# A low-rank product U^T x in an attention kernel with two mixers: taken once a batch over 512 columns, where it was taken once a pair of heads over 128

## The chip, the cores and the metric

The kernel runs on one core of a Trainium2 chip, as one program of 12022 instructions. The metric is the device time of one execution in microseconds. TensorE is called PE below, its loading of weights PEld, VectorE DVE, ScalarE ACT, GpSimd POOL, and the queue on which nearly all transfers are issued SP.

## The reference

A clustered attention is followed by two mixers. Batch 2, 8 heads, 768 tokens, head size 64, so 512 channels.

```python
scores = where(q_assign == k_assign, q @ k^T / 8, -1e9)      # clusters from an argmax against 16 centroids
x = softmax(scores) @ v                                       # laid out as (batch, 768 tokens, 512 channels)
# first mixer: U is 768 x 32, V is 32 x 768
h = x^T @ U @ V
u = x + h^T
x = u + relu(u @ w_ch1) @ w_ch2                               # 512 -> 2048 -> 512
# second mixer
h = relu(x^T @ w_tok1) @ w_tok2                               # 768 -> 256 -> 768
u = x + h^T
out = u + relu(u @ w_ch1') @ w_ch2'                           # 512 -> 1536 -> 512
```

The change concerns the first factor of the token mixing, z = U^T x: for each batch a 32 x 512 matrix (32 ranks by 512 channels), summed over 768 tokens.

## The kernel before, in words

The eight heads of a batch are worked as four pairs; a pair fills 128 channels. There are G = 8 pairs in all (g = 0 to 3 are batch 0, g = 4 to 7 batch 1). The attention of a pair is cut into 9 tiles (NTT), so the whole attention is 72 steps (`step`, L587). A step n runs the exponential of tile n on ACT (L298), the score matmuls of tile n+1 on PE (`st_mm`, L287, groups qS<-kS in the trace, printed as ps<-qS,kS), the units that find the row maxima of the next pair (`max_unit`, L246, printed as ps<-kS,qS, each with a maximum on DVE at L258 or L260), the product with v of tile n-1 (`pv`, L303, ps<-vt,p), and then the list `late[n]`, which is filled by hand with `at(late, s, ...)` from L525 on. Every engine works its own instructions in the order in which they are written, so this list is the schedule.

The result of the attention is divided and stored into `xn` (`pv_out`, L316), whose layout is 128 partitions (a token within a block) by batch, pair, token block (6 of them, NS) and 128 channels. It is float32.

The low-rank product of pair g is `zmm(g)` (L327): 6 matmuls, one for each token block, with a 128 x 32 block of U as the weights (`u_sb`) and the 128 channels of the pair moving. Both are plain float32, which the trace shows as two PE instructions for each matmul, 12 a pair. It is written into one bank of PSUM. `zmm_out(g)` (L334) then copies it twice on ACT, to partitions 0 to 31 and 32 to 63 of `zst` (L337, L338), and puts the remainder of the rounding into partitions 64 to 95 on DVE (L339, recorded at L88). With its three parts `zst` is the moving side of `zadd(b, t)` (L342), which multiplies with V and adds to `xn` (`zadd_out`, L345).

`zmm(g)` stands in `late` of step 9g+10, that is in the second step of the next pair, and `zmm_out(g)` in the step after it, for g = 0 to 6. The bank is 6 + g % 2, one of the two that `pv` uses in turn. The product of the last pair, g = 7, is the first entry of `rest_of_u` (L779), a list whose entries are taken in turn with half units of the first mixer's channel matmuls (`hidden`, `outmm`, L626 to L653: 12 matmuls of 512 columns each). There is one `zadd` for each of a batch's six token blocks: those of batch 0 stand in the steps of pairs 5 to 7 (L570), the first at step 49, those of batch 1 in `rest_of_u`, the first two entries after the product.

Besides, `tick` (L517) puts in the conversion of the weights of the mixers, which arrive as 64-bit words (`conv_all`, L477 on): two ACT instructions, four on DVE, one on POOL and two transfers each time.

The PE instructions of all these functions are issued by the helper `mm` (L75), so the trace has them all at L76; they are told apart by their tiles.

Of the kernel before, what the change touches and what calls it, by code (L numbers as in the profile page):

```python
# [18 lines left out]
P = 128  # L19
# [5 lines left out]
def tile_cluster_attention__then__two_mixers(  # L25
# [25 lines left out]
    NB, NPAIR, _, S = qT.shape  # L51
    HS = S // 2
    NS = S // P
    NT = HS // P
    D = 64
    CD = NPAIR * P
    NC = CD // P
    NFA, NFB = wa.shape[0], wb.shape[0]
    R = U.shape[1]
    DT = wt1.shape[1]  # L60
    NDT = DT // P
    G = NB * NPAIR
# [10 lines left out]
    ps = psp.tile([P, 8, 512], F32, name="ps")  # L73

    def mm(o, l, r, start, stop, **kw):  # L75
        pe.matmul(o, lhsT=l, rhs=r, start=start, stop=stop, **kw)  # L76
# [10 lines left out]
    def sub(eng, o, a, b):  # L87
        eng.tensor_tensor(out=o, in0=a, in1=b, op=ALU.subtract)  # L88
# [30 lines left out]
    xn = fp.tile([P, NB, NPAIR, NS, P], F32, name="xn")  # L119
# [38 lines left out]
    u_sb = const.tile([P, NS, R], F32, name="u_sb")  # L158
    vst = const.tile([96, S], F32R, name="vst")
    zst = const.tile([96, NB * CD], F32R, name="zst")  # L160
# [3 lines left out]
    def load_pair(g, eng=sp):  # L164
        b, p = divmod(g, NPAIR)
        eng.dma_start(Rq, qT[b, p])
        eng.dma_start(Rk, kT[b, p])

    def load_v(g):
        b, p = divmod(g, NPAIR)  # L170
        for a in range(2):
            sp.dma_start(vt[g % 2][:, a, :, 0:D], v[b].rearrange("(c s) d -> s c d", s=P)[:, :, p * P + a * D : p * P + a * D + D])
# [4 lines left out]
    def ring():  # L177

        banks.append(banks.pop(0))
        return banks[-1]  # L180

    held = {}

    def scores(g, bk=None):

        p = g % NPAIR
        held["sc"] = bk = ring() if bk is None else bk
        for qd in range(4):
            src = (Rq, Rk)[qd // 2]
            mm(ps[32 * qd : 32 * qd + 32, bk, 0:HS], zc[:, ts(p, 32)], src[:, ts(qd % 2, HS)], True, True)  # L190
# [28 lines left out]
    def q_lo(eng, o):  # L219
        eng.scalar_tensor_tensor(out=o.bitcast(F32R), in0=Rq, scalar=0.125, in1=Hq, op0=ALU.mult, op1=ALU.subtract)  # L220

    def k_lo(eng, o):
        sub(eng, o.bitcast(F32R), Rk, Hk)
# [22 lines left out]
    def max_unit(g, m):  # L246
        a, r = divmod(m, 9)
        q, k = qS[g % NST][a], kS[g % NST][a]
        bk = ring()
        tp, w = divmod(r, 3)  # L250
        for j, (t, k0, n) in enumerate([(2 * tp + w, 0, 512)] if w < 2 else [(2 * tp, 512, 256), (2 * tp + 1, 512, 256)]):
            o = ps[:, bk, j * n : j * n + n]
            mm(o, q[0:KA, 0, ts(t, P)], k[0:KA, 0, k0 : k0 + n], True, False)
            mm(o, q[0:KB0, 1, ts(t, P)], k[0:KB0, 1, k0 : k0 + n], False, True)
        i = 6 * a + 2 * tp
        mxs = mxs_[g % 2]
        if w < 2:
            dve.tensor_reduce(out=mxs[:, i + w, 0:1], in_=ps[:, bk, :], axis=AX.X, op=ALU.max, negate=True)  # L258
        else:
            dve.tensor_reduce(out=mxs[:, i : i + 2, 1], in_=ps[:, bk, :].rearrange("p (t k) -> p t k", t=2),  # L260
                              axis=AX.X, op=ALU.max, negate=True)

    def max_rows(g, tps=None, eng=sp):

        i, n = (0, NT) if tps is None else (tps, 1)
        parts = lambda t: t.rearrange("p (a t w) -> p a t w", a=2, w=2)[:, :, i : i + n]
        dve.tensor_reduce(out=parts(mxz[:, 0:12]), in_=mxs_[g % 2].rearrange("p (a t w) c -> p a t w c", a=2, w=2)[:, :, i : i + n],
                          axis=AX.X, op=ALU.min)
        bk = ring()
        mm(ps[:, bk, 0:P], mxz, ident, True, True)  # L270
        o = ps[0:12, bk, 0:P]
        m = mr[i % 2]
        rnd(dve, m[0:12, 0, :].bitcast(F32R), o)
        sub(dve, m[0:12, 1, :].bitcast(F32R), o, m[0:12, 0, :])
        for a in range(2):
            for j in range(2):
                d = f32(qS[g % NST][a])[96 + j : 97 + j, 1, i * QB : (i + n) * QB].rearrange("o (t s) -> o t s", s=P)
                eng.dma_start(d, m[6 * a + 2 * i : 6 * a + 2 * i + 2 * n, j, :])
# [22 lines left out]
    OB = 6  # L301
# [14 lines left out]
    def pv_out(k):  # L316
        g, qb = divmod(k, NQB)
        b, p = divmod(g, NPAIR)
        o = ps[:, OB + k % 2, 0 : 4 * VW].rearrange("p (a t x) -> p a t x", a=2, x=VW)
        r = rr[k % 2]  # L320
        dve.tensor_scalar(out=r, in0=o[:, :, :, D], scalar1=EPS, scalar2=None, op0=ALU.add)
        dve.reciprocal(r, r)
        dve.tensor_tensor(
            out=xn[:, b, p, ts(qb, 2), :].rearrange("p t (a d) -> p a t d", a=2), in0=o[:, :, :, 0:D],
            in1=r.unsqueeze(3).to_broadcast([P, 2, 2, D]), op=ALU.mult)

    def zmm(g, bk=None):  # L327
        b, p = divmod(g, NPAIR)
        held["z"] = bk = ring() if bk is None else bk
        z = ps[0:R, bk, 0:P]  # L330
        for c in range(NS):
            mm(z, u_sb[:, c, :], xn[:, b, p, c, :], c == 0, c == NS - 1)

    def zmm_out(g):  # L334
        z = ps[0:R, held["z"], 0:P]
        o = zst[:, ts(g, P)]
        act.copy(o[0:32], z)  # L337
        act.copy(o[32:64], z)  # L338
        sub(dve, o[64:96], z, f32(o[0:32]))  # L339
# [183 lines left out]
    early, mid, late, mus = {}, {}, {}, {}  # L523

    def at(d, s, f):  # L525
        d.setdefault(max(s, 0), []).append(f)

    for g in range(G):
        s0 = NTT * g
        for qb in range(NQB):  # L530
            at(late, s0 + 3 * qb + 3, lambda k=NQB * g + qb: pv_out(k))
        if g + 1 < G:
            at(late, s0 + 10, lambda g=g: zmm(g, OB + g % 2))
            at(late, s0 + 11, lambda g=g: zmm_out(g))
            n1 = g + 1
            cnt = (2, 2, 2, 2, 2, 2, 2, 2, 2) if g > 1 else (3, 3, 3, 3, 3, 3) if g else (0, 0, 0, 0, 0, 3, 4, 4, 4, 3)
            m0 = 0
            for s, k in zip(range((-2, 0, -3)[min(g, 2)], 8), cnt):
                for m in range(m0, m0 + k):
                    at(mus, s0 + s, lambda g=n1, m=m: max_unit(g, m))  # L540
                m0 += k
            at(mid, s0 + (6 if g else 7), lambda g=n1: max_rows(g))
        if g + 2 < G:
            n2 = g + 2
            at(late, s0 - (4 if g > 1 else 3), lambda g=n2: load_pair(g))
            at(late, s0 + 10, lambda g=n2: load_v(g))
            s1 = s0 - 1 if g else 3
            at(late, s1 - 1, lambda g=n2, bk=OB + (3 * g if g else 1) % 2: scores(g, bk))
            at(late, s1 - 1, q_hi)
            at(late, s1, k_hi)  # L550
            at(late, s1, scores_out)
            at(late, s1, argmax_a)
            at(late, s1 + 1, argmax_b)
            at(late, s1 + 1, lambda: k_lo(pool, Rk))
            for a in range(2):
                at(late, s1 + 1, lambda g=n2, a=a: stack(g, a, "hi", sp))
                at(late, s1 + 3, lambda g=n2, a=a: stack(g, a, "lo", sp))
                at(late, s1 + 3, lambda g=n2, a=a: stack(g, a, "mask", sp))
            at(late, s1 + 2, mask_rows)
            at(late, s1 + 2, lambda: q_lo(dve, Rq))  # L560
        for s in (2, 4, 6) if g else (7, 8):
            at(late, s0 + s, tick)
# [7 lines left out]
    for t in range(NS):  # L570
        g, qb = 5 + t // 2, t % 2
        s, bk = NTT * g + 3 * qb + 4, OB + (NQB * g + qb) % 2
# [206 lines left out]
    def rest_of_u():  # L779


        ops = [(lambda bk: zmm(G - 1, bk), lambda bk: zmm_out(G - 1))]
        u_ = [(umm, umm_out, 0, t) for t in range(TW // P, NS)] + [(umm, umm_out, 1, t) for t in range(NS)]
        z_ = [(zadd, zadd_out, 1, t) for t in range(NS)]
        order = [x for p in zip(u_, z_) for x in p] + u_[NS:]
        for f, o, b, t in order:
            ops.append((lambda bk, f=f, b=b, t=t: f(b, t, bk), lambda bk, o=o, b=b, t=t: o(b, t, bk)))
        for i in range(len(ops) + 1):
            if i:
                ops[i - 1][1](6 + (i - 1) % 2)  # L790
            if i < len(ops):
                ops[i][0](6 + i % 2)
            yield
# [4 lines left out]
    def conv_rest():  # L798
        for k in range(2 * len(blocks)):
            if k % 9 % 2 or k % 9 == 0:  # L800
                tick()
            yield

    bg = [rest_of_u(), conv_rest()]
    while done < end(0, 2) - 24:
        for t in bg:
# [48 lines left out]
```

## Time and profile before

| | us |
|---|---|
| three runs | 866.0, 862.29, 870.77 (median 866.0) |
| the profiled execution's own time | 862.45 |
| its span in the trace | 860.4 |
| PE busy in the span | 815.7 |
| DVE, ACT, POOL busy | 457.5, 239.2, 121.1 |

The span is the time from the first to the last instruction of the profiled execution; about 2.0 us lie around it. A duration of a PE matmul in the trace holds the passage through the array, so successive matmuls overlap: the distance from one start to the next is what it costs the engine. In a timeline a row is a run of like instructions, with its start, its length and its count; an idle time before it stands in brackets, with what ended it. The granted clock is PE's share of its full 2.4 GHz: 0.50 is the lower level of 1.2 GHz, 1.00 the higher.

### The profile page before, as it was taken

The numbers are of one execution on the slowest core, as the hardware profiler recorded it, in microseconds if no ns is written. First come the engines' busy times: TensorE is split into PE (matmuls) and PEld (weight loads), VectorE is DVE, ScalarE is ACT, GpSimd is POOL, SyncE is SP. The second block draws the span as 40 slices with busy tenths as digits, with TensorE's granted clock in tenths as the row PEclk, the third lists the DMA queues.
The fourth block names the chain that finished last, engine by engine and source line by source line (L and its number), as shares of the span: only waits on it lengthen the run. The fifth ranks groups of instructions, "written<-read, shape, count | busy, mean of one in ns | idle before, by whom it ended". The sixth has DMA issues, their size and how long they took to land.

```text
span 860.4 us, 12022 instructions
## 1 busy us (share of the span) xinstructions
PE 815.7 (95%) x4585; PEld 702.6 (82%) x4585; DVE 457.5 (53%) x795; ACT 239.2 (28%) x367; POOL 121.1 (14%) x103
## 2 busy tenths in 40 slices
PE   0779899999999999999999999999999999999997
PEld 0668799999989999788888888888888888888886
DVE  3746667676767545877877588751242124113113
ACT  1221333434333334433323333321211121111010
POOL 3000001102111011212312332310210021000000
PEclk9998899999999999999999999999999999999999
DMA  8554735677774436799989999973454345754852
GB/s 212 126 118 127 164 111 139 200 168 220 179 191 133 165 101 208 284 358 333 376 292 321 416 388 417 402 265 137 130 171 166 127 130 162 250 193 163 275 191 80
DMA packets 70505, 184.72 MB, mean 215 GB/s; under 512 B 21776, under 2 KB 24016, under 8 KB 70448
## 3 DMA queue, kind: packets, MB, share of 16 engines
q1 hardware_dynamic: 69232, 181.83, 65.1%
q10 hardware_dynamic: 1216, 2.14, 1.0%
q8 instruction: 36, 0.59, 0.3%
q14 instruction: 21, 0.17, 0.1%
HBM read 130.88 MB, written 32.51 MB: 190 GB/s over the span
## 4 chain that ended last, share of the span: by engine, by line
PE 88%; DVE 5%; DMA 4%; SPq 2%; issue 1%; ACT 0%; ACTq 0%; DVEq 0%
PE ps L76 87%; DMA sq__101<-in_qT_dram 2%; DVE mxs L258 1%; DMA kS<-sk__102 1%; PE ps L731 1%; DMA whl<-scr_a 1%; DMA kS<-om 0%; PE ps L351 0%; SPq L239 0%; DMA cc<-in_cen_dram 0%; SPq L240 0%; DVE xn L663 0%; DVE mxs L260 0%; DVE ul L88 0%; DVE am L199 0%
## 5 line engine op out<-in xcount | busy, mean ns | idle before, releaser
L76 PE MATMUL ps<-uh,whl 128*128 128x512 f32 x672 | 223.1, 393 | 0.9 <-issue 0.9
L76 PE MATMUL ps<-gh,whl 128*128 128x512 f32 x672 | 222.1, 392 | 0.0
L641 DVE SCALAR_TENSOR_TENSOR gl<-ps,gh 128x512 fp32r<-128x512 f32 x84 | 58.0, 690 | 220.5 <-ACT gh L640 220.5
L76 PEld LDWEIGHTS ps<-uh,whl 128*128 128x128 f32 x672 | 126.2, 188 | 28.0 <-issue 1.1
L76 PEld LDWEIGHTS ps<-gh,whl 128*128 128x128 f32 x672 | 126.2, 188 | 27.2
L76 PE MATMUL ps<-vt,p 128*128 128x65 f32 x1152 | 138.6, 274 | 0.0
L76 PEld LDWEIGHTS ps<-vt,p 128*128 128x128 f32 x1152 | 137.2, 194 | 0.2
L76 PE MATMUL ps<-ul,whl 128*128 128x512 f32 x336 | 132.0, 393 | 1.0 <-DVE ul L88 1.0
L76 PE MATMUL ps<-gl,whl 128*128 128x512 f32 x336 | 132.0, 393 | 0.0
L640 ACT ACTIVATE gh<-ps 128x512 fp32r<-128x512 f32 x84 | 50.2, 598 | 288.7 <-PE ps L76 288.7
L88 POOL TENSOR_TENSOR chl<-c,chl 128x512 fp32r<-128x512 f32 x56 | 76.0, 1358 | 334.7 <-ACT chl L81 300.6
L298 ACT ACTIVATE p<-ps 128x1024 f32<-128x1024 f32 x72 | 73.2, 1021 | 136.9 <-PE ps L76 136.8
L76 PE MATMUL ps<-kS,qS 112*128 112x512 f32 (+3 forms) x384 | 87.0, 360 | 23.2 <-DMA kS<-om 17.0
L76 PE MATMUL ps<-qS,kS 112*128 112x256 f32 x576 | 98.6, 297 | 1.0 <-DMA qS<-mr 1.0
L258 DVE TENSOR_REDUCE mxs<-ps 128x1 f32<-128x512 f32 x96 | 63.6, 684 | 61.0 <-PE ps L76 60.8
L76 PEld LDWEIGHTS ps<-qS,kS 112*128 112x128 f32 x576 | 83.5, 195 | 11.5 <-issue 2.8
L76 PEld LDWEIGHTS ps<-kS,qS 112*128 112x128 f32 (+1 forms) x384 | 62.1, 202 | 32.6 <-issue 18.5
L76 PEld LDWEIGHTS ps<-ul,whl 128*128 128x128 f32 x336 | 63.2, 188 | 14.2 <-DVE ul L88 1.3
L76 PEld LDWEIGHTS ps<-gl,whl 128*128 128x128 f32 x336 | 63.2, 188 | 13.0
L81 ACT ACTIVATE chl<-c 128x512 fp32r<-128x512 f32 x56 | 35.3, 631 | 58.3 <-DMA scr_a<-chl 25.0
L107 DVE SCALAR_TENSOR_TENSOR c<-c,c 128x512 int32<-128x512 int32 (+1 forms) x63 | 47.4, 752 | 2.2
L106 DVE TENSOR_SCALAR c<-c 128x512 int32<-128x512 int32 (+1 forms) x63 | 45.7, 725 | 2.1
(113 smaller groups left out, 575.1 us busy)
## 6 DMA issues: line engine op xcount, KB each, us to landing
whl<-scr_a SPq DMA_DIRECT2D x96, 512.0 KB
whl<-scr_b SPq DMA_DIRECT2D x72, 512.0 KB
c<-in_wa_dram SPq DMA_DIRECT2D x32, 512.0 KB
scr_a<-chl SPq DMA_DIRECT2D x32, 512.0 KB
c<-in_wb_dram SPq DMA_DIRECT2D x24, 512.0 KB
scr_b<-chl SPq DMA_DIRECT2D x24, 512.0 KB
qS<-sq__101 SPq DMA_DIRECT2D x15, 384.0 KB
kS<-sk__102 SPq DMA_DIRECT2D x29, 192.0 KB
```

Of the source, the lines that this page charges most:

```text
L76: pe.matmul(o, lhsT=l, rhs=r, start=start, stop=stop, **kw)
L81: act.activation(o, i, AF.Copy, scale=scale)
L88: eng.tensor_tensor(out=o, in0=a, in1=b, op=ALU.subtract)
L106: dve.tensor_scalar(out=d, in0=d, scalar1=3, scalar2=0x3FFFFFF8, op0=ALU.logical_shift_left, op1=ALU.bitwise_and)
L107: dve.scalar_tensor_tensor(out=d, in0=lo, scalar=29, in1=d, op0=ALU.logical_shift_right, op1=ALU.bitwise_or)
L258: dve.tensor_reduce(out=mxs[:, i + w, 0:1], in_=ps[:, bk, :], axis=AX.X, op=ALU.max, negate=True)
L298: act.activation(p32[n % NP32].rearrange("p (i k) -> p i k", i=2), ps[:, b0 : b0 + 2, :], AF.Exp)
L640: act.activation(gh, o, AF.Relu)
L641: dve.scalar_tensor_tensor(out=gl, in0=o, scalar=0.0, in1=f32(gh), op0=ALU.max, op1=ALU.subtract)
L731: pe.transpose(ps[:, k, ts(c, P)], x2[:, c, b * S + s * P : b * S + s * P + P], ident)
```

## The change

`zmm` takes a batch instead of a pair: 6 matmuls, with the same 128 x 32 blocks of U as weights and all four pairs' channels, 512 columns, moving, into a whole bank of PSUM. `zmm_out` takes the 32 x 512 result in the same three instructions, each four times as wide. The calls for g = 0, 1, 2, 4, 5 and 6 go away; the call at step 37 (after pair 3) does batch 0, and the first entry of `rest_of_u` does batch 1. The rest is the same.

```diff
-    def zmm(g, bk=None):
-        b, p = divmod(g, NPAIR)
-        held["z"] = bk = ring() if bk is None else bk
-        z = ps[0:R, bk, 0:P]
+    def zmm(b, bk):
+        z = ps[0:R, bk, :]
         for c in range(NS):
-            mm(z, u_sb[:, c, :], xn[:, b, p, c, :], c == 0, c == NS - 1)
-    def zmm_out(g):
-        z = ps[0:R, held["z"], 0:P]
-        o = zst[:, ts(g, P)]
+            mm(z, u_sb[:, c, :], xn[:, b, :, c, :], c == 0, c == NS - 1)
+    def zmm_out(b, bk):
+        z = ps[0:R, bk, :]
+        o = zst[:, ts(b, CD)]
         act.copy(o[0:32], z)
         act.copy(o[32:64], z)
         sub(dve, o[64:96], z, f32(o[0:32]))
...
         if g + 1 < G:
-            at(late, s0 + 10, lambda g=g: zmm(g, OB + g % 2))
-            at(late, s0 + 11, lambda g=g: zmm_out(g))
+            if g == NPAIR - 1:
+                at(late, s0 + 10, lambda g=g: zmm(0, OB + g % 2))
+                at(late, s0 + 11, lambda g=g: zmm_out(0, OB + g % 2))
...
     def rest_of_u():
-        ops = [(lambda bk: zmm(G - 1, bk), lambda bk: zmm_out(G - 1))]
+        ops = [(lambda bk: zmm(1, bk), lambda bk: zmm_out(1, bk))]
```

## Rows read from the trace of the kernel before

**Rows 1.** The page: busy time of each engine with its share of the span, and the chain that ended last by engine.

```profile
PE 815.7 (95%) x4585; PEld 702.6 (82%) x4585; DVE 457.5 (53%) x795; ACT 239.2 (28%) x367; POOL 121.1 (14%) x103
PE 88%; DVE 5%; DMA 4%; SPq 2%; issue 1%; ACT 0%; ACTq 0%; DVEq 0%
```

**Rows 2.** Busy time of the engines in stretches of the span. Columns: stretch, its length, PE, PEld, DVE, ACT and POOL busy (with instructions), the granted clock of PE, the busy share of the DMA engines, GB/s.

```profile
101.80:108.70 6.90, 6.90 (x29) 5.75 (x29) 1.78 (x3) 1.19 (x3) 0.00 (x0) 0.51 0.27 62
108.70:120.00 11.30, 11.30 (x89) 10.82 (x89) 7.41 (x15) 3.62 (x4) 0.00 (x0) 1.00 0.61 196
120.00:345.00 225.00, 222.40 (x1776) 210.93 (x1776) 145.85 (x296) 88.30 (x115) 31.73 (x23) 1.00 0.60 164
345.00:349.50 4.50, 2.54 (x18) 1.94 (x17) 4.36 (x10) 3.13 (x6) 1.27 (x1) 1.00 0.65 255
349.50:856.00 506.50, 506.23 (x2280) 418.20 (x2278) 237.98 (x351) 118.15 (x210) 75.59 (x59) 1.00 0.70 252
```

**Rows 3.** The waits of PE's matmuls from 108 to 345 us, all that the view has: who waited for whom, us in total, times, the longest.

```profile
PE ps L76 <- DVE mxz L267: 2.6, 5, 0.5
```

**Rows 4.** The same view as Rows 2 for two whole pairs of heads, each of 9 steps, from exponential to exponential.

```profile
135.96:172.77 36.81, 36.29 (x288) 34.02 (x288) 25.86 (x53) 14.59 (x19) 5.70 (x4) 1.00 0.65 178
172.77:209.58 36.81, 36.29 (x288) 34.02 (x288) 25.83 (x53) 14.56 (x19) 5.69 (x4) 1.00 0.73 189
```

**Rows 5.** PE in order of time from 140 us: one step with a product and the steps after it. The rows qS,kS 112x256 with four instructions open a step.

```profile
141.10 0.73 PE L76 MATMUL ps<-qS,kS 112*128 112x256 f32 x4
...
144.93 1.50 PE L76 MATMUL ps<-xn,u_sb 128*32 128x128 f32 x12
146.35 0.75 PE L76 MATMUL ps<-qS,kS 112*128 112x256 f32 x4
...
150.09 0.73 PE L76 MATMUL ps<-qS,kS 112*128 112x256 f32 x4
...
153.78 0.73 PE L76 MATMUL ps<-qS,kS 112*128 112x256 f32 x4
...
157.49 0.72 PE L76 MATMUL ps<-qS,kS 112*128 112x256 f32 x4
```

**Rows 6.** PE at 103 us: the first product, in the stretch of the lower clock.

```profile
103.45 2.77 PE L76 MATMUL ps<-xn,u_sb 128*32 128x128 f32 x12
106.15 1.22 PE L76 MATMUL ps<-qS,kS 112*128 112x256 f32 x4
```

**Rows 7.** DVE in the same place.

```profile
108.27 1.43 DVE L258 TENSOR_REDUCE mxs<-ps 128x1 f32<-128x512 f32 x2 [5.10 <-PE ps L76]
```

**Rows 8.** All instructions of one form: their count, and the shortest, median and longest duration in ns.

```profile
L76 PEld LDWEIGHTS ps<-xn,u_sb x96: 106/110/177, 103.5 to 352.7; 128*32 128x32 f32 x96
L76 PE MATMUL ps<-xn,u_sb x96: 272/273/423, 103.5 to 352.9; 128*32 128x128 f32 x96
L76 PE MATMUL ps<-sq__101,zc x32: 486/510/849, 7.4 to 243.7; 128*32 128x384 f32 x32
```

**Rows 9.** PE at the cluster scores of a pair: plain float32 too, 32 columns of weights and 384 moving, four side by side in four quarters of the array, and each in two instructions, one set after the other.

```profile
243.34 0.52 PE L76 MATMUL ps<-sq__101,zc 128*32 128x384 f32 x2
...
243.69 0.49 PE L76 MATMUL ps<-sq__101,zc 128*32 128x384 f32 x2
```

**Rows 10.** From the chain of waits in order of time: one half unit of the mixer, 12 matmuls of 512 moving columns in the rounded type (fp32r).

```profile
556.52 2.76 PE ps L76 x12
```

**Rows 11.** Groups of instructions of one shape. After the bar: busy time in us, mean duration in ns, idle time before them.

```profile
L337 ACT CAST zst<-ps 32x128 fp32r<-32x128 f32 x8 | 2.0, 256 | 20.5 <-PE ps L76 20.5
L88 DVE TENSOR_TENSOR zst<-ps,zst 32x128 fp32r<-32x128 f32 x8 | 2.3, 282 | 4.8 <-ACT zst L338 4.6
L732 ACT CAST xnh<-ps 128x512 fp32r<-128x512 f32 x12 | 7.0, 585 | 14.2 <-PE ps L731 14.2
L88 DVE TENSOR_TENSOR xnl<-ps,xnh 128x512 fp32r<-128x512 f32 x12 | 8.2, 685 | 6.5 <-ACT xnh L732 6.5
```

**Rows 12.** ACT in order of time around the product of pair 3, which is the place of batch 0's product after the change.

```profile
220.08 0.26 ACT L337 CAST zst<-ps 32x128 fp32r<-32x128 f32 x1 [2.08 <-PE ps L76]
220.35 0.26 ACT L338 CAST zst<-ps 32x128 fp32r<-32x128 f32 x1
220.63 0.63 ACT L81 ACTIVATE chl<-c 128x512 fp32r<-128x512 f32 x1
221.17 0.66 ACT L99 ACTIVATE c<-c 128x512 f32<-128x512 f32 x1
222.26 1.03 ACT L298 ACTIVATE p<-ps 128x1024 f32<-128x1024 f32 x1 [0.43 <-PE ps L76]
```

**Rows 13.** PE in order of time at the last product and the first `zadd` of batch 1.

```profile
351.63 1.50 PE L76 MATMUL ps<-xn,u_sb 128*32 128x128 f32 x12
353.06 0.65 PE L351 MATMUL ps<-ident,xn 128*128 128x128 f32 x4
...
356.31 0.39 PE L76 MATMUL ps<-zst,vst 96*128 96x512 f32 x1
```

**Rows 14.** ACT in the same place.

```profile
353.16 0.26 ACT L337 CAST zst<-ps 32x128 fp32r<-32x128 f32 x1 [0.83 <-PE ps L76]
```

## The prediction

> **What bounds the kernel now.** I read the page's engine line and chain first [rows 1]: PE is busy for 815.7 of 860.4 us and makes 88% of the chain that ended last, with DVE at 5% and DMA at 4%. A busy PE can still be one that waits in small pieces, so the stretches come next [rows 2]. From 108.7 us on PE has work without a break at a granted clock of 1.00, the higher level: 222.4 of 225 us in the attention and 506.2 of 506.5 us in the mixers. The list of its matmuls' waits from 108 to 345 us has one entry, 2.6 us in five pieces behind DVE's mxz [rows 3]. DVE, the next engine, is busy for 25.9 of the 36.8 us of a pair [rows 4]. So after 108.7 us a microsecond of PE work taken out of the attention or the mixers is a microsecond off the end, and one put in is one more.
>
> The low-rank product is PE work. What it costs is best read from the distance of the steps, not from its own duration [rows 5]. The groups that open a step start at 141.10, 146.35, 150.09, 153.78 and 157.49 us: 5.25, 3.74, 3.69 and 3.71 us apart. The first step holds a product. Against 3.69 it is 1.56 us longer, and with the 3.74 behind it 1.6; I take 1.59. Of this 1.42 lies between the product's first start and the next group's (144.93 to 146.35), and the rest is the switch into it.
>
> **The change part by part: how much of the cost is columns.** If the 12 instructions of a product were limited by something paid once an instruction (loading weights, issue), then the same 12 with 512 columns would cost little more, and six of eight products would be saved almost whole. If they are limited by the columns that stream through, nothing is saved but the switches, since 8 x 12 x 128 and 2 x 12 x 512 columns are the same 12288.
>
> The rows have the same kind of instruction (float32, 32 columns of weights) at two widths [rows 8]: 128 columns last 272 ns at the shortest, 384 columns 486 ns. 256 more columns cost 214 ns, 0.836 ns a column. The two sets of the 384-column scores start 0.35 us apart [rows 9], which is 384 x 0.836 = 0.32 and a little. For 128 columns it gives 107 ns, and the 12 starts of a product lie (1.50 - 0.27)/11 = 0.112 us apart [rows 5]. So a product is limited by its columns already, with some 5 ns an instruction beside them, though weight loads of 110 ns [rows 8] are as long and could hide behind the same number; at 128 columns alone the two can't be told apart, and it is the 384-column rows that decide.
>
> A 512-column instruction then takes 384 x 0.836 = 321 ns more than a 128-column one, and a product of 12 takes 3.85 us more: 1.59 + 3.85 = 5.44 us. The bounds from rows: downward, 0.23 us an instruction, as 12 instructions of 512 columns in the rounded type take 2.76 us [rows 10]; upward, 384 columns at 0.35 us from start to start scaled to 512, 0.47 us. The middle value of 0.433 is nearest to the same type's rows, and I keep it.
>
> The Trainium skill has a rule that speaks for a much larger gain. "TensorE: Matmul & The Clock Gate", section Back-to-back issue gap, gives for streams of weight load and matmul some 81 ns a matmul at 128 columns and 131 ns at 512, 1.6 times for four times the columns. By it a wide product would be far below four narrow ones. The 384-column rows speak against it here, with 486 against 272 ns.
>
> **The removed products.** Five of them, those of pairs 1, 2, 4, 5 and 6, lie behind 108.7 us in stretches where PE never waits: 5 x 1.59 = 7.95 us. That of pair 0 is apart. It runs from 103.45 to 106.15 us [rows 6], at the lower level [rows 2], 2.70 us. DVE waits for PE for 5.10 us right behind it [rows 7], so PE is what is late there, and taking it out moves on what follows. But the work that moves up runs at the lower level itself: if the clock comes back at 108.7 us as now, 2.70 us gained there are worth 1.35 us, with the switch some 1.5. The bounds are 1.35 and, if the denser work brings the clock back sooner, 2.70 and half of the 2.55 us that are left of that stretch, 4.0. I take 1.5. What is late next in the steps without a product is PE still: DVE has 25.6 us of work in 35.2 (a pair less 1.59 us, without the 0.28 of the remainder).
>
> **The two wide products.** At step 37 and at the head of the mixers' list a narrow product is replaced by a wide one: 2 x 3.85 = 7.70 us more, all on PE and all on the path.
>
> **The way out.** The three instructions of the way out become four times as wide and a quarter as many. Same kinds at 512 columns take 585 ns on ACT and 685 ns on DVE, against 256 and 282 [rows 11]. In total ACT goes from 16 x 0.256 = 4.1 to 4 x 0.585 = 2.3 us and DVE from 2.3 to 1.4; neither is on the path, so I count nothing. The wide copies can delay what is queued behind them. At step 38 ACT has two copies, two conversions and then the exponential, which waited 0.43 us for PE [rows 12]; the copies take 2 x 0.33 = 0.66 us longer, so the exponential starts some 0.2 us late. Its result is wanted a step later, 3.7 us on. In the mixers the copies start 0.10 us after PE went on to its transposes [rows 13, 14], and `zadd` comes 3.25 us after that point. Two copies and the remainder take 0.10 + 1.17 + 0.69 = 1.96 us. So `zadd` doesn't wait; without that cover it would cost at most the 2 us. The bank that the product fills is wanted by `pv` at step 40 only. No transfer is added, moved or issued in another order.
>
> **The sum.** -7.95 - 1.5 + 7.70 = -1.75, say -1.8 us, against the profiled execution's own 862.45 us (span 860.4 and 2.0 around it): 860.7 us. This execution is at the low end of what is shown, with 862.29, 866.0 and 870.77 beside it. The middle of the four is (862.45 + 866.0)/2 = 864.2, and for a median of new runs I take that less 1.8: 862.4 us.
>
> **The rivals.** *The columns are cheap.* The pace of narrow products is that of loading weights, and the wide instruction runs at the 0.23 us of the rounded type. A wide product is then 1.59 + 12 x (0.23 - 0.112) = 3.0 us, the two add 2.8 in place of 7.7, and the sum is -6.6: 857.6 us. For it is the 110 ns weight load, as long as the pace; against it the 384-column rows. By the ratio of 1.6 of the Trainium skill's page it would be about -7.8.
>
> *The clock falls in a wide product: slower.* For 5.2 us PE would do nothing but 32-column work, a quarter of the array. No stretch of before has more than 1.5 us of it at the higher level, and the only product at the lower level (103.45 us) lies in a stretch of 6.9 us of that clock. If the granted clock falls to 0.50 during or behind a wide product for a stretch of that length, then work of half of it is lost, 3.45 us each time. It decides from one such fall on: -1.8 + 3.45 = +1.7, or 865.9 us, and with both +5.1, 869.3 us. Against it: from 108.7 us on the granted clock is 1.00 throughout, even in 345 to 349.5 us, where PE is busy for 2.5 of 4.5 us [rows 2]. The same page of the Trainium skill (TensorE: Matmul & The Clock Gate, section Part 4: PE-mode transpose) says that transposes don't engage the higher level as other matmuls do. The row of 345 us, which holds transposes and idle time, shows no fall, and no run here shows long 32-column work.
>
> *The change doesn't do what it says.* The moving side is four pieces of 128 channels that don't lie side by side. If each matmul were cut at the pieces, 96 instructions would remain, only the six switches (about 0.2 us each) and the lower clock's 0.2 would be saved: -1.4 us, 862.8 us. The count of instructions tells it at once.
>
> **How the numbers follow.** My forecast has 0.66, the cheap columns 0.13, the fallen clock 0.13, the uncut form 0.04, and 0.04 is left for what I don't see. The range goes from the cheap columns, 857.6 us and a little below for a low run, to the case of two falls, 869.3 us; within it the executions' own spread of 8.5 us is the larger part. I give 857.0 to 869.0; the bounds of the terms alone fill 857.6 to 863.3 (0.23 and 0.47 us an instruction give -6.6 and -0.9, the first product's bounds -1.6 and -4.3). A change of 1% is 8.7 us, about what a measurement of this kernel can tell from none. Faster by that needs the cheap columns and a good run together: 0.08. Slower by it needs both falls and a bad run: 0.04. The rest, 0.88, is the same within 1%.
>
> **What would show it.** The group ps<-xn,u_sb should stand with 24 instructions of 512 columns at about 0.43 us from start to start and a duration near 0.59 us, in two blocks of 5.1 to 5.3 us. Steps of pairs 1, 2, 4, 5 and 6 that were 5.25 us should be 3.7. A pair without a product should last 35.2 us instead of 36.8, the one with the wide product 40.7. The pace of 0.23 us would prove me wrong on the columns; a stretch at 0.50 behind a wide product would prove the third case; a wait of PE in the steps that lost a product would show that DVE or a transfer took over, which I exclude. The prediction is wrong if the time differs by more than 5 us from before.

## The result, and the profile after

The changed kernel is slower. 13 runs of each on the same chips have medians of 883.48 us after and 868.87 us before; the ratio is 1.0143, 95% interval 1.0114 to 1.0172, and the time lies outside the forecast range of 857.0 to 869.0 us. This ratio and those of the experiments leave out executions more than 1.5% above their kernel's fastest; here those are the ones that were longest at the lower clock (up to 936.76 us), so the ratio is, if anything, low. The profiled execution took 884.78 us (span 882.3), 22 us more than that of before.

The page of the changed kernel, first the engines' busy time, then PE's granted clock in 40 slices (9 stands for 90% or more):

```profile
PE 838.7 (95%) x4513; PEld 716.0 (81%) x4513; DVE 458.5 (52%) x789; ACT 236.8 (27%) x355; POOL 121.7 (14%) x103
PEclk9978579879999999999999999999999999999999
```

PE has 72 instructions fewer than in [rows 1] and is busy for 23 us more. The third to ninth slices tell why: the clock. In stretches (columns as in [rows 2]):

```profile
85.60:123.10 37.50, 36.25 (x149) 32.25 (x149) 17.68 (x28) 11.09 (x13) 1.82 (x1) 0.50 0.57 151
123.10:170.90 47.80, 46.05 (x358) 43.27 (x359) 33.45 (x65) 16.09 (x20) 5.68 (x4) 1.00 0.46 123
170.90:188.00 17.10, 17.09 (x75) 14.85 (x74) 6.94 (x16) 4.81 (x6) 3.09 (x2) 0.50 0.73 203
188.00:365.50 177.50, 171.22 (x1344) 160.03 (x1342) 113.76 (x229) 69.40 (x87) 24.54 (x18) 1.00 0.57 164
365.50:368.90 3.40, 3.40 (x8) 2.65 (x9) 2.32 (x4) 0.00 (x0) 0.23 (x1) 0.50 0.38 154
```

In [rows 2] the clock was at 1.00 from 108.7 us to 856 us. Now it is at the lower level for 37.5 us in the start, for 17.1 us inside the attention and for 3.4 us at the change to the mixers.

The wide product itself is as forecast. All its instructions (the answer to [rows 8]), PE around the first of the two ([rows 5]), and ACT behind it ([rows 12]):

```profile
L76 PE MATMUL ps<-xn,u_sb x24: 592/592/617, 234.1 to 374.5; 128*32 128x512 f32 x24
```

```profile
234.13 5.34 PE L76 MATMUL ps<-xn,u_sb 128*32 128x512 f32 x12
239.40 0.75 PE L76 MATMUL ps<-qS,kS 112*128 112x256 f32 x4
```

```profile
239.50 0.58 ACT L336 CAST zst<-ps 32x512 fp32r<-32x512 f32 x1 [5.92 <-PE ps L76]
...
241.81 1.00 ACT L298 ACTIVATE p<-ps 128x1024 f32<-128x1024 f32 x1
```

24 instructions, 592 ns each; 5.27 us from the first start to the next group, and 1.42 + 3.85 = 5.27 follows from the terms of the prediction. The exponential follows the conversions without its idle time of before, and PE doesn't wait for it here. The clock was at 1.00 through both wide products (234 and 370 us).

What is new stands among the waits of PE from 120 to 355 us. The second row is that of [rows 3]; the first had no counterpart:

```profile
PE ps L76 <- ACT p L298: 4.0, 3, 1.6
PE ps L76 <- DVE mxz L267: 2.1, 4, 0.5
```

PE now waits three times for an exponential, once in each of the pairs 2, 3 and 5. It is a wait for room: the scores of tile n+1 go into the two banks of PSUM from which the exponential of tile n-1 reads (`st_mm`, `softmax`). How the wait comes about is read in pair 2 from the views of ACT, PE, SP and DVE. ACT before, then ACT after, from the exponential of the pair's fifth step on:

```profile
152.34 1.02 ACT L298 ACTIVATE p<-ps 128x1024 f32<-128x1024 f32 x1 [2.67 <-PE ps L76]
157.74 0.63 ACT L81 ACTIVATE chl<-c 128x512 fp32r<-128x512 f32 x1 [4.38 <-DMA scr_a<-chl]
...
158.84 1.93 ACT L298 ACTIVATE p<-ps 128x1024 f32<-128x1024 f32 x2
```

```profile
159.48 1.02 ACT L298 ACTIVATE p<-ps 128x1024 f32<-128x1024 f32 x1 [2.67 <-PE ps L76]
167.62 0.63 ACT L81 ACTIVATE chl<-c 128x512 fp32r<-128x512 f32 x1 [7.11 <-DMA scr_a<-chl]
...
168.70 1.92 ACT L298 ACTIVATE p<-ps 128x1024 f32<-128x1024 f32 x2
```

ACT's rounding of converted weights (L81, in a tick) has to wait until one of the two chl buffers has been written to scratch, and the exponentials behind it on ACT wait too. Before, the wait was 4.38 us and already held the next exponential until 158.84 us; with its 1.02 us it ended at 159.86, and PE opened the step whose scores go into its banks at 161.20:

```profile
161.20 0.73 PE L76 MATMUL ps<-qS,kS 112*128 112x256 f32 x4
```

That was a cover of 1.3 us that no wait of PE showed. In pairs 3, 4 and 5 the same distance was 1.4, 0.9 and 0.2 us. After, the wait is 7.11 us and PE stands still:

```profile
166.63 1.90 PE L76 MATMUL ps<-vt,p 128*128 128x65 f32 x16
169.76 0.75 PE L76 MATMUL ps<-qS,kS 112*128 112x256 f32 x4 [1.23 <-ACT p L298]
```

Two things moved against each other. PE's steps come 1.59 us earlier without the narrow product. And the write itself came later: on SP it stands behind the 13 transfers of the next pair's stacks, at 0.63 us each, which begin when DVE has finished L211 and L220. SP before and after, the first stack transfer and the write:

```profile
146.28 0.52 SPq L235 DMA_DIRECT2D qS<-sq__101  x1
...
154.45 0.58 SPq L507 DMA_DIRECT2D scr_a<-chl  x1
```

```profile
156.09 0.52 SPq L235 DMA_DIRECT2D qS<-sq__101  x1
...
164.27 0.58 SPq L506 DMA_DIRECT2D scr_a<-chl  x1
```

The 8.2 us between them are the same. But counted from the exponential of the pair's second step (139.66 and 148.37 us) the first transfer is at 6.6 us before and 7.7 after, because DVE's L211 took 0.46 us before and 1.56 after. DVE before, then DVE after:

```profile
144.93 0.46 DVE L211 TENSOR_SCALAR om<-ohT,msk 128x384 f32<-128x384 bf16 x1
```

```profile
153.64 1.56 DVE L211 TENSOR_SCALAR om<-ohT,msk 128x384 f32<-128x384 bf16 x1
```

POOL's share of the conversion, which used to come later (147.72 us, after L211), ran beside it. It follows ACT's rounding, and that came earlier: before, ACT's rounding stood behind the two copies of the way out, which wait for PE [rows 12], and these copies are gone. ACT and POOL after:

```profile
153.00 0.62 ACT L81 ACTIVATE chl<-c 128x512 fp32r<-128x512 f32 x1
```

```profile
153.70 1.29 POOL L88 TENSOR_TENSOR chl<-c,chl 128x512 fp32r<-128x512 f32 x1 [9.21 <-ACT chl L81]
```

In pairs 3 and 5 POOL began a little later beside DVE, and there it is the next instruction that was long, L220 with 2.05 us in place of 0.95:

```profile
197.88 2.05 DVE L220 SCALAR_TENSOR_TENSOR sq__101<-sq__101 128x768 fp32r<-128x768 f32 x1
```

All traces of this case agree. From the start of L211 to the end of L220 it is 2.39 to 2.43 us in each of the 24 places, in eight traces, where this POOL instruction runs beside them, and 1.32 to 1.35 us in the 46 others that begin after 90 us.

1.6 us earlier on PE and 1.1 later on ACT, against a cover of 1.3: a wait of 1.2 to 1.4, and 1.23 is what PE's row has. From 170.9 us, 1.2 us after this wait, the clock is at 0.50 for 17.1 us.

By the starts of the exponentials, the whole execution in us (a pair is 9 steps; the third column is the first experiment, told below):

| | before | after | e1 |
|---|---|---|---|
| start, to step 18 | 136.0 | 144.7 | 146.6 |
| pair 2 | 36.8 | 43.9 | 35.2 |
| pair 3 | 36.8 | 36.6 | 35.3 |
| pair 4 (wide product) | 36.8 | 40.6 | 40.6 |
| pair 5 | 36.4 | 36.6 | 34.8 |
| pair 6 | 32.7 | 31.1 | 31.1 |
| pair 7, to its last exponential | 23.8 | 22.3 | 22.3 |
| rest (wide product) | 521.1 | 526.5 | 525.0 |

### The profile page after: what moved, and what is told of

It is laid out like the page before. It is cut to its first block, busy times and chain, and to the rows that moved or that the text cites. A ratio compares the mean times of both kernels' runs of the same rounds, so it can differ in the third digit from the quotient of the medians.

```text
span 882.3 us, 11853 instructions
## 1 busy us (share of the span) xinstructions
PE 838.7 (95%) x4513; PEld 716.0 (81%) x4513; DVE 458.5 (52%) x789; ACT 236.8 (27%) x355; POOL 121.7 (14%) x103
## 4 chain that ended last, share of the span: by engine, by line
PE 82%; DMA 5%; DVE 5%; SPq 5%; issue 1%; ACT 1%; ACTq 0%; DVEq 0%
PE ps L76 81%; DVE mxs L258 1%; DMA sq__101<-in_qT_dram 1%; SPq L240 1%; SPq L239 1%; DMA scr_a<-chl 1%; DMA kS<-sk__102 1%; DMA vt<-in_v_dram 1%; DVE sq__101 L220 1%; PE ps L731 1%; SPq L236 1%; SPq L235 0%; DMA whl<-scr_b 0%; DMA kS<-om 0%; DVE xn L663 0%
## 5 line engine op out<-in xcount | busy, mean ns | idle before, releaser
L76 PE MATMUL ps<-vt,p 128*128 128x65 f32 x1152 | 148.8, 286 | 0.0
L76 PEld LDWEIGHTS ps<-vt,p 128*128 128x128 f32 x1152 | 147.8, 207 | 0.2
L76 PE MATMUL ps<-kS,qS 112*128 112x512 f32 (+3 forms) x384 | 93.5, 380 | 18.8 <-DMA kS<-om 15.0
L76 PE MATMUL ps<-qS,kS 112*128 112x256 f32 x576 | 104.6, 311 | 5.1 <-ACT p L298 4.0
L76 PEld LDWEIGHTS ps<-qS,kS 112*128 112x128 f32 x576 | 89.5, 209 | 17.1 <-ACT p L298 5.6
L76 PEld LDWEIGHTS ps<-kS,qS 112*128 112x128 f32 (+1 forms) x384 | 67.1, 218 | 28.7 <-issue 16.5
L81 ACT ACTIVATE chl<-c 128x512 fp32r<-128x512 f32 x56 | 35.2, 629 | 59.3 <-DMA scr_a<-chl 24.7
L107 DVE SCALAR_TENSOR_TENSOR c<-c,c 128x512 int32<-128x512 int32 (+1 forms) x63 | 48.4, 767 | 2.2
L108 DVE SCALAR_TENSOR_TENSOR c<-c,c 128x512 int32<-128x512 int32 (+1 forms) x63 | 44.2, 701 | 2.2
```

The lines of the kernel that those rows point to most:

```text
L81: act.activation(o, i, AF.Copy, scale=scale)
L107: dve.scalar_tensor_tensor(out=d, in0=lo, scalar=29, in1=d, op0=ALU.logical_shift_right, op1=ALU.bitwise_or)
L108: dve.scalar_tensor_tensor(out=d, in0=hi, scalar=-0x40000000, in1=d, op0=ALU.bitwise_and, op1=ALU.bitwise_or)
```

## The experiments

Four theories were set against each other: A, the new wait of PE behind the exponential and the fall of the clock behind it; B, the fall comes from the missing products as such; C, the start, where pair 0's product is gone; D, the wide products. Ratios are to the kernel before on the same chip; times in us are medians over all runs of a kernel.

**The waits taken away.** e1 gives the changed kernel a third buffer, so that ACT's rounding has nothing to wait for.

```diff
-    chl = [fp.tile([P, 2, 512], F32R, name=f"chl_{i}") for i in range(2)]
+    chl = [fp.tile([P, 2, 512], F32R, name=f"chl_{i}") for i in range(3)]
...
-                o = chl[k % 2]
+                o = chl[k % 3]
```

> The changed kernel with three buffers instead of two for the converted weights (chl), so that ACT's rounding in a tick doesn't wait for the write to scratch that stands behind the thirteen transfers of the next pair's stacks on SP. Theory A (a new wait: without the narrow products PE reaches the scores before the exponential that is queued on ACT behind that rounding; PE idles 1.2 to 1.6 us a pair and the clock falls behind it): no wait of PE for ACT's exponential from 124 to 355 us, granted clock 1.00 there, time 1.8 us below the kernel before, ratio about 0.998. Theory B (the clock falls because the narrow products themselves are gone as PE work, wait or not): stretches at 0.50 remain in the attention and the ratio stays at 1.010 or above. Theory C (the start: without pair 0's product the lower level lasts until 123 us): the stretch at 0.50 from 86 to 123 us remains, ratio about 1.01. Theory D (the wide products bring the fall): 0.50 behind them, ratio 1.01.

Measured: 870.02 us against 866.09, ratio 1.0042 (1.0003 to 1.0080). PE's waits from 120 to 345 us are those of [rows 3] again, one row, and the stretches are:

```profile
84.60:129.00 44.40, 43.09 (x178) 38.88 (x178) 20.07 (x33) 12.00 (x14) 1.83 (x1) 0.50 0.50 141
129.00:345.00 216.00, 213.38 (x1673) 199.45 (x1673) 144.25 (x285) 85.57 (x105) 32.41 (x23) 1.00 0.59 162
```

The products are gone and the clock in the attention stays at 1.00: B falls, D too. From step 18 on the execution is 724.3 us long against 724.4 before, where -7.95 + 7.70 = -0.25 was worked out for these parts. The long stretch in the start is still there: C is not out, and the ratio lies between the 0.998 of A alone and the 1.01 of C.

e2 is the control, the same third buffer in the kernel before.

> The kernel before with the third chl buffer alone. Theory A: in the kernel before the wait of ACT is there (4.4 us at 154 us) but doesn't reach PE, so nothing is won: ratio 0.997 to 1.002. If the third buffer itself changed the time through other ways (conversion, transfers), this shows it. Theories B, C and D: the same ratio of 1.000.

Measured: 863.75 us, ratio 0.9986 (0.9960 to 1.0013). The buffer alone wins nothing that can be told from none.

e7 takes the same wait away in another way: the pair's first tick one step earlier, so that its write is issued ahead of the stacks.

```diff
-        for s in (2, 4, 6) if g else (7, 8):
+        for s in (1, 4, 6) if g else (7, 8):
```

> The changed kernel with two chl buffers, and the first of the three ticks of a pair one step earlier, so that its write to scratch is issued on SP ahead of the 13 transfers of the stacks and not behind them. Another way to take the same wait away. Theory A: no wait of PE for the exponential from 124 to 355 us, granted clock 1.00 there, ratio as with the third buffer, 1.000 to 1.008. Theory B (the missing products as such): falls remain, 1.010 or above.

Measured: 866.47 us, ratio 1.0000 (0.9961 to 1.0039), no wait for the exponential, clock 1.00 from 104.7 to 345 us.

**The products put back.** e3 adds to the changed kernel the narrow products of five pairs as work that nobody reads; e4 adds that of pair 0 alone.

```diff
+    def zdummy(g):
+        b, p = divmod(g, NPAIR)
+        z = ps[0:R, OB + g % 2, 0:P]
+        for c in range(NS):
+            mm(z, u_sb[:, c, :], xn[:, b, p, c, :], c == 0, c == NS - 1)
...
+            if g in (1, 2, 4, 5, 6):        # e4: (0,)
+                at(late, s0 + 10, lambda g=g: zdummy(g))
```

> The changed kernel with the narrow products of pairs 1, 2, 4, 5 and 6 put back at their places as work whose result nobody reads, beside the two wide ones. It adds 5 x 1.59 = 7.95 us of PE work to the changed kernel. Theory A: the waits behind the exponential and the falls in the attention vanish; +6.1 us against the kernel before, ratio 1.007, and so faster than the changed kernel by some 6 us though it does more. Theory B: the same. Theory C: the long start remains, so 1.014 plus 0.009, less what the attention gives back: 1.015 to 1.02. Theory D (the wide products): 1.02 or above.

Measured: 878.07 us over four runs, ratio 1.0108 (1.0021 to 1.0195). Eight microseconds more work than the changed kernel, and 5 us less by the medians, which four runs can't tell from none (the intervals of the two ratios overlap). One wait of 0.5 us was left and no fall in the attention (granted clock 1.00 from 117.3 to 345 us; the profiled execution took 873.96 us). It is above the 1.007 that theory A gave, but the interval holds both that and C's 1.015, so it doesn't settle the start.

e3 also takes the two movements apart, since it has the products but not their copies on ACT. L211 takes 1.54 us here too, and in pair 2 the exponential's row on ACT and that of the step on PE which needs its banks are:

```profile
162.98 1.92 ACT L298 ACTIVATE p<-ps 128x1024 f32<-128x1024 f32 x2
```

```profile
164.22 0.73 PE L76 MATMUL ps<-qS,kS 112*128 112x256 f32 x4
```

The first of the two exponentials ends at 164.00, so 0.2 us of the cover of 1.3 is left: the delay of the write takes 1.1 us of it by itself, and the time that PE gains without the product does the rest.

> The changed kernel with the narrow product of pair 0 alone put back (11th step) as work whose result nobody reads. Theory C (the start): the lower level ends near 109 us as in the kernel before, and the time goes back to within 0.3% of the kernel before. Theories A and B: the waits and falls in the attention remain; time within 0.4% of the changed kernel's, ratio 1.010 to 1.018.

Measured: 879.39 us, ratio 1.0132 (1.0096 to 1.0168): no recovery, so pair 0's product isn't the larger cause. Its trace is the best view of the falls. PE's three waits for the exponential, then the stretches:

```profile
161.35 0.75 PE L76 MATMUL ps<-qS,kS 112*128 112x256 f32 x4 [1.18 <-ACT p L298]
```

```profile
197.99 0.87 PE L76 MATMUL ps<-qS,kS 112*128 112x256 f32 x4 [1.19 <-ACT p L298]
```

```profile
279.97 0.92 PE L76 MATMUL ps<-qS,kS 112*128 112x256 f32 x4 [1.58 <-ACT p L298]
```

```profile
198.50:208.70 10.20, 10.19 (x42) 9.31 (x42) 4.98 (x13) 3.24 (x5) 1.28 (x1) 0.50 0.54 195
208.70:280.40 71.70, 69.59 (x522) 61.80 (x522) 48.43 (x92) 25.71 (x32) 10.30 (x7) 1.00 0.64 162
280.40:290.60 10.20, 10.19 (x42) 9.31 (x41) 4.84 (x12) 2.65 (x4) 1.27 (x1) 0.50 0.35 130
```

The clock falls 0.5 and 0.4 us after the second and the third wait end. After the first it doesn't.

**The wait brought into the kernel before.** e9 leaves all eight narrow products where they were and moves the second tick of pairs 1 to 5 one step up, so that ACT stands at its rounding one exponential sooner.

```diff
-        for s in (2, 4, 6) if g else (7, 8):
+        for s in ((2, 3, 6) if 0 < g < 6 else (2, 4, 6)) if g else (7, 8):
```

> The kernel before, all eight narrow products at their places, with the second tick of pairs 1 to 5 one step earlier (step 3 of the pair in place of 4). ACT then stands at its rounding, behind the same write to scratch, one exponential earlier, so the wait that the kernel before hides should reach PE without any product being taken away. Theory A: PE waits 1 to 3 us for the exponential in most of the five pairs, the clock falls behind some of these waits; ratio 1.010 to 1.030. Theory B (the fall needs the products gone): waits of PE of 5 to 12 us at most, clock 1.00 in the attention, ratio 1.006 to 1.014 by the waits alone.

Measured: 910.92 us, a median of four runs (893.78 to 913.86) against 866.81. Three of its four waits of PE, and the stretches:

```profile
163.86 1.22 PE L76 MATMUL ps<-qS,kS 112*128 112x256 f32 x4 [2.23 <-ACT p L298]
```

```profile
207.33 0.75 PE L76 MATMUL ps<-qS,kS 112*128 112x256 f32 x4 [2.22 <-ACT p L298]
```

```profile
293.88 1.22 PE L76 MATMUL ps<-qS,kS 112*128 112x256 f32 x4 [2.54 <-ACT p L298]
```

```profile
163.80:174.00 10.20, 10.14 (x41) 9.56 (x42) 2.42 (x4) 3.02 (x5) 1.27 (x1) 0.50 0.40 151
...
208.20:225.30 17.10, 17.09 (x74) 16.12 (x72) 7.11 (x16) 4.14 (x6) 1.27 (x1) 0.50 0.34 121
...
293.50:303.70 10.20, 9.82 (x40) 9.24 (x41) 2.70 (x5) 3.34 (x5) 1.54 (x2) 0.50 0.26 106
```

The four waits are 9.5 us together (the fourth, 2.46 us at 254.03, has no fall behind it). The time is above the 1.030 of the expectation, 27 us over the kernel before at the lowest run, which is the profiled one, and 44 at the median. Its pairs 2 to 5 are 26.1 us longer than before: 9.5 are the waits, and 16.6 go with the 37.5 us at the lower level. So the wait suffices, with no product taken away.

e12 is the changed kernel once more, for a second profile of it.

> The changed kernel as it is, for a second profile of it. Theory A: three to five waits of PE of 1.2 to 1.6 us for the exponential between 124 and 355 us as in the first profile, a stretch at 0.50 directly behind at least one of them, not necessarily the same one; time 872 to 890 us. If the falls have nothing to do with the waits, the stretches begin elsewhere.

Measured: 882.77 us, ratio 1.0154 (1.0102 to 1.0205). The profiled execution took 937.54 us. It has three waits, 3.9 us in all; two of them, and the stretches that go with them:

```profile
160.92 1.22 PE L76 MATMUL ps<-qS,kS 112*128 112x256 f32 x4 [1.18 <-ACT p L298]
```

```profile
283.97 1.23 PE L76 MATMUL ps<-qS,kS 112*128 112x256 f32 x4 [1.48 <-ACT p L298]
```

```profile
160.70:181.20 20.50, 20.27 (x86) 17.85 (x86) 8.02 (x18) 6.11 (x9) 3.21 (x3) 0.50 0.72 205
181.20:283.60 102.40, 99.06 (x751) 89.92 (x750) 71.96 (x138) 36.78 (x46) 14.07 (x10) 1.00 0.61 159
283.60:420.10 136.50, 135.38 (x593) 130.88 (x594) 44.40 (x92) 32.84 (x42) 10.70 (x9) 0.50 0.27 95
```

A wait of 1.48 us was followed by 136.5 us at the lower level; the start of this execution was short, 3.4 and 6.8 us. Such stretches are the likely source of the changed kernel's spread (872.53 to 937.54 us): its mean clock falls from 0.976 in the shortest execution to 0.901 in the longest. Only two executions of it have a trace.

What a fall costs is read from pairs with one such wait each. They last 36.6 us without a fall (pair 3 after, pair 2 in e4), 40.7 with 10.2 us at 0.50 (pair 3 in e4), 43.9 with 17.1 (pair 2 after) and 45.0 with 20.5 (pair 2 in e12): some 0.4 us for each microsecond at the lower level.

**The start.** e5 takes both suspects away: the third buffer and pair 0's product put back.

> The changed kernel with three chl buffers and the narrow product of pair 0 put back at its place (11th step) as work whose result nobody reads: both suspects taken away together. Theory C (what the third buffer alone left, ratio 1.0042, is the start, where the absence of pair 0's product lets the lower clock last longer): it costs 1.6 us and gives back 4 to 10 us in the start; ratio 0.997 to 1.001. Rival E (the start's stretch at the lower level is a draw that falls alike with and without the product): 1.6 us on top of the third buffer's 1.0042, ratio 1.005 to 1.007.

Measured: 867.03 us, ratio 0.9994 (0.9966 to 1.0021), inside C's range and below the rival's. e6 goes the other way: the kernel before with the third buffer, all products narrow, pair 0's taken 12 steps later.

```diff
-            at(late, s0 + 10, lambda g=g: zmm(g, OB + g % 2))
-            at(late, s0 + 11, lambda g=g: zmm_out(g))
+            at(late, s0 + (10 if g else 22), lambda g=g: zmm(g, OB + g % 2))
+            at(late, s0 + (11 if g else 23), lambda g=g: zmm_out(g))
```

> The kernel before with three chl buffers, all eight products narrow, but that of pair 0 taken 12 steps later (step 22 in place of 10). The work is the same. Theory C: the start's stretch at the lower level gets longer as in the changed kernel; ratio 1.003 to 1.007 against the kernel before, most executions at a clock of 0.972 or below. Rival E: as with the third buffer alone, 0.9986, within 0.997 to 1.001.

Measured: 872.79 us against 868.69, 4 us more for the same work by the medians; the ratio is 1.0021 (0.9987 to 1.0055), between the two ranges of the expectation, and its interval reaches into both. The stretch in the start of its profile, then that of e5 with the product that ran in it:

```profile
84.60:129.00 44.40, 43.26 (x179) 38.88 (x179) 20.02 (x33) 11.99 (x14) 1.82 (x1) 0.50 0.51 141
```

```profile
86.40:113.70 27.30, 26.03 (x109) 22.18 (x108) 13.78 (x22) 8.76 (x10) 1.84 (x1) 0.50 0.54 141
```

```profile
111.09 2.77 PE L76 MATMUL ps<-xn,u_sb 128*32 128x128 f32 x12
```

With the product in its place the long stretch ended as the product did; without it, it lasted 15 us more. One trace of each decides little, since e12's start was short without the product. The mean clocks of all executions say more. Over the kernels without the exponential's wait it was 0.970 or less in 13 of 32 runs without pair 0's product in the start (4 of 10 in e1, 6 of 12 in e6, 3 of 10 in e7) and in none of 99 with it (before, e2, e5). This mark was chosen after the runs; at the 0.972 of e6's expectation it is 16 of 32 against 24 of 99, and e6 itself has 6 of 12, which isn't "most". So C holds as a matter of chances. Its price is less sure: some 4 us by the medians of e1 and e6, 2 us and not told from none by e6's ratio. Why this product shortens the stretch stays open.

**A version that beats both.** e8 is e1 with 12 more instructions of the product's kind in step 7, ahead of the cluster scores, where PE waits for a transfer just before the start's long stretch.

```diff
+    def zfill(bk):
+        z = ps[0:R, bk, 0:P]
+        for i, c in enumerate((0, 1, 2, 3, 0, 1)):
+            mm(z, u_sb[:, c, :], xn[:, 0, 0, c, :], i == 0, i == 5)
...
+            if g == 1:
+                at(late, s1 - 1, lambda: zfill(OB + 1))
```

> The changed kernel with three chl buffers and 12 more instructions of the product's kind (128 columns, result unread) in step 7, ahead of the cluster scores, where PE waits 0.5 us for a transfer just before the stretch at the lower level that begins at 84.6 us. They last 1.3 us. If that stretch starts because PE stands still there, it is gone or short: 2 to 10 us won for 0.8 to 1.3 us, ratio 0.993 to 1.000. If not, ratio 1.005 to 1.006.

Measured: 863.56 us, ratio 0.9966 (0.9935 to 0.9998). The ratio is inside the first range of the expectation. PE's wait for the transfer is gone in the profile, and the stretch still begins (3.4 us at 84.9), so this wait isn't what begins it; but the long one is rare: a mean clock of 0.972 in one of ten runs and more in the others. e10 is the kernel before with the same two edits, e11 is e8 again, on one chip with twelve runs each.

> The kernel before with three chl buffers and the filling work ahead of the cluster scores in step 7. With the next run it measures what the change itself is worth when neither the wait nor the start is in the way. If the sum of the columns and switches holds: 1.8 us above the changed kernel with the same two edits, ratio 0.998 to 1.000 against the kernel before; most executions at a clock of 0.982 or more.

> The changed kernel with three chl buffers and the filling work, once more with more rounds, beside its counterpart of the kernel before on the same chip: ratio 0.995 to 0.999 against the kernel before, and 1 to 2.5 us below the counterpart. If the earlier 0.9966 was a lucky draw of starts: 1.000 or above.

Measured: e10 865.0 us, ratio 0.9986 (0.9966 to 1.0007); e11 863.61 us, ratio 0.9955 (0.9933 to 0.9977). e11 beats both kernels, the one before by less than half a per cent. The change itself is worth 1.4 us in it by the medians, near the forecast's 1.8 (1.8 by the means, 95% interval 0.8 to 2.8 from the twelve runs each). For the kernel before the filling work does nothing that shows: 0.9986 with it (e10) and without (e2).

## Why the prediction was wrong, point by point

- **Columns limit the product: right.** 24 instructions, 592 ns and 0.43 us apart, 5.27 us a wide product, as worked out. The cheap columns and the cut moving side are out.
- **The sum of products and switches: right where nothing else interferes.** Pairs of 35.2 and 40.6 us (35.2 and 40.7 forecast), -0.1 us from step 18 on in e1 (-0.25), -1.4 us in all between e10 and e11 (-1.8).
- **The way out: right for the wide copies, wrong for those that went away.** The first exponential behind the wide copies came without idle time, nobody waited for it, and PE went on to `zadd` without a wait. But "neither is on the path, so I count nothing" left out what stands behind the narrow copies on ACT: without them its rounding came 2.7 us earlier in the pair, POOL ran beside DVE, and the write to scratch was 1.1 us later in pairs 2 and 3 (0.2 us in pair 5).
- **"What is late next in the steps without a product is PE still": this step failed.** It rested on DVE's busy time [rows 4] and on PE having no waits [rows 3]. Neither shows how near a wait is. The exponential of the pair's sixth step had a cover of 0.2 to 1.4 us, less than the 1.59 that the change took from PE's time, and ACT, busy for only 28%, stood still for 4.4 us and more there in the kernel before. The prediction worked out such covers at the two wide products (3.7 and 3.25 us), and none in the steps that lose a product. In its place the runs showed three waits of PE for ACT, 4.0 us in all, and the lower clock behind them. The text said that it excluded a transfer taking over in these steps; it was a write to scratch, through ACT.
- **No transfer is "issued in another order": true, and not enough.** The order on SP was the same; the first stack transfer was 1.1 us later in the step because DVE's instructions ahead of it ran beside POOL, in all 24 places with that overlap and in none without.
- **The fallen clock: near in its price for a microsecond (0.5, against 0.4), wrong in place and length.** It was put behind the wide products, where the clock stayed at 1.00. The trace of before was read for the clock after PE's waits at 345 us, 0.94 and 1.02 us long, where no fall showed. That was a draw: behind the same two waits the clock fell for 3.4 us in 9 of the 13 traces in which it was at 1.00 until there, four of them kernels with all narrow products (e2, e6, e9, e10). The falls that cost the time are behind the new waits of 1.2 to 2.5 us, and their length, taken as 6.9 us, was 10 to 136 us.
- **The first product: wrong sign.** Its removal was booked at 1.5 us won. With it gone the start's stretch at the lower level is longer in more runs, which costs some 2 to 4 us by e1 and e6.

The larger part, then, is the wait and the clock behind it: taking it away brings 1.0143 down to 1.0042 (e1) or 1.0000 (e7); taking both away brings 0.9994 (e5).

## What to carry to other kernels

Before taking work out of the engine that is never idle, look for the smallest cover around it: how long before it is wanted does each input arrive and each buffer come free, also from engines that are mostly idle, and what waits ahead of it in its own queue. Work that goes away lets what stood behind it run earlier, on every engine that had a part in it; ask what it will then run beside. A microsecond taken from PE is won only where every cover is larger than that microsecond. And where PE runs at the higher clock, a new wait is not priced at its own length: here, with some 4 us of waits in each trace of the changed kernel, its executions were 4 to 70 us over the median of before, some of it from the start.

## What the runs showed of the hardware that was not expected

PE waits of 1.2 to 2.5 us were followed by the lower clock in most cases: behind one of three in the first profile of the changed kernel, two of three in e4 and e12, three of four in e9, beginning within 1.2 us of the wait's end (in some rows up to 0.4 us before it). Behind two shorter ones close together, 0.94 and 1.02 us at the change to the mixers, it fell in 9 of 13 traces. A busy PE does not bring the clock back soon: in e12 it was busy for 135.4 of 136.5 us at 0.50. The Trainium skill ("TensorE: Matmul & The Clock Gate", section What's actually happening) says that activity releases the throttle; that row shows that this can take very long. What sets the length wasn't found.

DVE's L211 of 0.46 us took 1.56 us with POOL's instruction of 1.29 us begun 0.06 us behind it (153.64 us); where POOL began 0.11 us behind it, L211 was not longer, and the next, L220, took 2.05 us in place of 0.95 (197.88 us).
